# Training step of a parallel attention and SwiGLU block: copies joined, operand tiles kept in a ring, and a 64-row partial product issued beside the score pair

## The chip, the cores and the metric

The kernel runs on one core of a Trainium2 chip, in one launch. A NeuronCore has five engines with an instruction queue each: PE (matrix multiply), ACT (ScalarE), DVE (VectorE), POOL (GpSimd) and SP (which here only issues DMAs). Each engine works through its queue in order, and engines wait for each other by semaphores. The metric is device time in microseconds (us); lower is better. "Before" is the median of three runs.

## The reference

For x, dy of 2048 rows and 448 features (bfloat16), with 16 heads of 28 features and an FFN of 1792:

```
xn  = (x - mean) / sqrt(var + 1e-5)                # no gain, no bias
out = x + softmax(q k^T / sqrt(28)) v @ wo         # q, k, v = heads of xn @ wqkv
        + (silu(xn @ w_gate) * (xn @ w_up)) @ w_down
```

The outputs are `out` and the gradients of it, for the incoming `grad_out` (dy), with respect to x, wqkv, wo, w_gate, w_up and w_down.

## The kernel before

The 16 heads are 4 groups (`g`) of 4 heads; a head is padded from 28 to 32 rows, so a group fills 128 partitions. Rows of the sequence are 16 tiles (`t`) of 128. The 448 features are three chunks of 128 and one of 64 that is filled up with zeros; `xn_sp` and `dy_sp` hold rows with 512 columns, `xnT` and `dyT` the transposed chunks, and the weights `wq_sb`, `wgu`, `wdT` four chunks each with zeros in rows 64 to 127 of the last.

**Prologue.** x is loaded and normalised in four blocks (`ln_stats`, `ln_rows`), transposed on PE (`ln_columns`), and group 0 is projected (`proj_block`).

**Forward** (loop over `steps`: 4 groups, 4 query chunks `qc` of 512, 16 key tiles `kt`, so 256 steps). A step has two halves. In each, two score matmuls of 32 rows (L554) fill a two-bank PSUM tile and ACT takes its exp (L558). After the first half PE does the four PV matmuls of the step before last (`pv`, L536). Then `fill(pace)` issues other work from `queue` up to a budget, `pace = left / steps to go`: the FFN products (gate `a`, up `u`, and `dh` against dy; four 512-column matmuls each, L362), the weight gradients (`dW_items`, 16 matmuls of 448 columns each, L336), the projections of the next group (`proj_items`), and what follows from a finished query chunk (`o_items`). Each item is a list of (cost, function) pairs; `cur` is the one under way. The products and weight gradients share three PSUM buffers `f_ps`; DVE and ACT take the results out. Transposed copies are made by DMA; operands of the backward go to DRAM (`qT_d`, `spq_d` and so on), as do the FFN's hidden values and gradients (`hd_d`). After the last step the rest of the queue is issued and the forward's pools are closed.

**Backward** (loop over 512 `units` in 64 windows of 8; a unit is a pair of heads, a key chunk `kc` of 512 and a query tile). `load_pair` and `load_group` bring a pair's and a group's operands from DRAM, two buffers each (`qdp`, `spg`). Unit k: two score matmuls (L821, rows 0 to 63), two matmuls for d of the unit before (L834, rows 64 to 127), exp on ACT (L839), ds = d * E on DVE (L851), and four accumulating matmuls for the unit three back (`acc_mm`, L714). Six of eight ds tiles in a window are transposed by DMA, two (`TQ`) on PE into `aux` (L741): one at position 6 and one at position 0 of the next window. `tr_out` copies each out, the first half by ACT (L748), the second by DVE (L750). Each window also has one entry of `jobs` in positions 1 to 4, which needs the only `aux` buffer: a row tile of `out` (`y`, 21 matmuls), a row tile of the FFN's input gradient (`dx`, 14), a piece of the gradient of wqkv (`dwq`), or none. Position 5 has the dq matmuls (`dq_mm`).

**End.** The last group's `dwq`, then for each row tile 14 matmuls that sum the parts of the gradient of xn (`pab` and `dq_c`), and the LayerNorm's backward: `g_sb`, `junk`, `bb`, `cc` and `t2` on DVE, `t1` on ACT, `dx` on POOL, and the store.

All order is written out by hand (`manual_schedule`); the tile pools place the semaphores.

Of the kernel before, what the change touches and what calls it, by code (L numbers as in the profile page):

```python
# [37 lines left out]
def kernel(  # L38
# [53 lines left out]


    bst = ExitStack()
    bp = bst.enter_context(tc.tile_pool(name="bp", bufs=1))
    osp = bst.enter_context(tc.tile_pool(name="osp", bufs=2))
# [7 lines left out]
    qkp = bst.enter_context(tc.tile_pool(name="qkp", bufs=2))  # L104
    vp = bst.enter_context(tc.tile_pool(name="vp", bufs=1))
    stg = bst.enter_context(tc.tile_pool(name="stg", bufs=1))
    ep = bst.enter_context(tc.tile_pool(name="ep", bufs=7))
    op_ = bst.enter_context(tc.tile_pool(name="op_", bufs=1))
# [18 lines left out]
    for c, (d0, dn) in enumerate(DCH):  # L127
        act.dma_start(out=wst[:dn, c, :], in_=A_wqkv[d0:d0 + dn, :])
# [7 lines left out]
    dve.memset(xn_sp[:, :, D:], 0.0)  # L136
    dve.memset(wq_sb[64:, 3], 0.0)
# [4 lines left out]
    for w in wgu:  # L142
        pool.memset(w[64:, :, 3, :], 0.0)
    pool.memset(wd3[:, :, 64:], 0.0)
    pool.memset(dy_sp[:, :, D:], 0.0)
# [3 lines left out]
    for c, (d0, dn) in enumerate(DCH):  # L149
        pool.tensor_copy(  # L150
            out=wq_sb[:dn, c].rearrange("p t g (hh r) -> p t (g hh) r", r=HP)[:, :, :, :DH],
            in_=wst[:dn, c, :].rearrange("p (t h d) -> p t h d", t=3, h=H))

    def load_ffn_w(fc):
        w, fs = wgu[fc % 2], slice(fc * P, (fc + 1) * P)
        q = sp if fc < 2 else pool
        for i, src in enumerate((B_w_gate, B_w_up)):
            q.dma_start(out=w[:, i, 0:3, :], in_=src[0:384, fs].rearrange("(c p) f -> p c f", p=P))
            q.dma_start(out=w[:64, i, 3, :], in_=src[384:448, fs])
        sp.dma_start_transpose(out=wdT[fc % 2][:, 0:3, :], in_=B_w_down[fs, 0:384])  # L160
        sp.dma_start_transpose(out=wdT[fc % 2][:, 3:4, :], in_=wd3[:, fc, :])

    sp.dma_start(out=wd3[:, :, 0:64], in_=B_w_down[:, 384:448].rearrange("(fc p) d -> p fc d", p=P))
    load_ffn_w(0)
    for b in range(2):
        sp.dma_start(out=dy_sp[:, 8 * b:8 * b + 8, :D], in_=dy_d[:, 8 * b:8 * b + 8, :])
# [8 lines left out]

    def proj_unit(g, tq, sc, evac):

        key = (g, tq)
        if sc == 0:
            qk_tiles[key] = (vp if tq == 2 else qkp).tile([P, S], BF16, name=("qT", "kT", "vT")[tq])  # L180
        dst = qk_tiles[key]
        pp = ps_f.tile([P, 512], FP32, name="f_ps")

        def mm(c):
            pe.matmul(pp[:], lhsT=wq_sb[:, c, tq, g, :], rhs=xnT[:, 4 * sc:4 * sc + 4, c, :],
                      start=(c == 0), stop=(c == 3))
            if c < 3:
                return
            o = dst[:, sc * 512:(sc + 1) * 512]
            if tq == 0:  # L190
                if evac == "act":
                    act.copy(out=o, in_=pp[:])
                else:
                    dve.tensor_copy(out=o, in_=pp[:])
            elif evac == "act":
                act.activation(out=o, in_=pp[:], func=ACT.Identity, bias=r_ones[:, 0:1], scale=1.0)
            else:
                dve.tensor_scalar(out=o, in0=pp[:], scalar1=r_ones[:, 0:1], scalar2=None, op0=ALU.add)
        return mm
# [26 lines left out]
    def ln_rows(b):  # L226
        bs = slice(4 * b, 4 * b + 4)
        dve.reciprocal(out=rstd[:, bs], in_=rstd[:, bs])
        for t in range(4 * b, 4 * b + 4):
            dve.tensor_scalar(out=xn_sp[:, t, :D], in0=x_b[b][:, t % 4, :],  # L230
                              scalar1=mv[:, t, 0:1], scalar2=rstd[:, t:t + 1],
                              op0=ALU.subtract, op1=ALU.mult)

# [38 lines left out]
    spp = fst.enter_context(tc.tile_pool(name="spp", bufs=2))  # L272
    def weight_layout(c, i):
# [5 lines left out]
               else wq_sb[:dn, c].rearrange("p t g r -> p (t g r)"))  # L279
# [6 lines left out]
    cur = deque()  # L286
    left = [0.0]

    def fill(budget):

        while budget > 0.05:
            if not cur:
                if not queue:
                    return
                cur.extend(queue.popleft())
            cost, fn = cur.popleft()
# [3 lines left out]

    def push(jobs, front=False):
        left[0] += sum(c for job in jobs for c, _ in job)
# [5 lines left out]
    def proj_items(g):  # L308
        out = []
        for tq in range(3):  # L310
            for sc in range(4):
                box = {}

                def go(c, tq=tq, sc=sc, box=box):
                    if c == 0:
                        box["m"] = proj_unit(g, tq, sc, "dve")
                    box["m"](c)
                out.append([(MM, lambda c=c, go=go: go(c)) for c in range(4)])
# [36 lines left out]
    def ffn_items(fc, sc, extra):  # L355
# [3 lines left out]
        def mm(name, w, src, c):  # L359
            if c == 0:  # L360
                st[name] = ps_f.tile([P, 512], FP32, name="f_ps")
            pe.matmul(st[name][:], lhsT=w(c), rhs=src[:, tsl, c, :], start=(c == 0), stop=(c == 3))  # L362

        def a(c):
# [4 lines left out]
            mm("a", lambda c: wgu[fc % 2][:, 0, c, :], xnT, c)  # L369
# [12 lines left out]
        def u(c):  # L382
            mm("u", lambda c: wgu[fc % 2][:, 1, c, :], xnT, c)
# [7 lines left out]
        def dh(c):  # L391
            mm("dh", lambda c: wdT[fc % 2][:, c, :], dyT, c)
# [11 lines left out]
        def four(f):  # L404
            return [(MM, lambda c=c: f(c)) for c in range(4)]
        return [four(a), four(u)] + extra + [four(dh)]
# [3 lines left out]
    for fc in range(NFC):  # L410
        nxt = dW_items(fc)
        for sc in range(4):
            ffn_list += ffn_items(fc, sc, pend[sc - 1:sc] if sc else [])
# [4 lines left out]
        pend = nxt  # L418
    ffn_list += pend
# [25 lines left out]
    def o_items(g, qc, o_ps):  # L445
# [5 lines left out]
        if qc == 0:  # L451
            O_sp[g] = osp.tile([P, NT, P], BF16, name="O_sp")
# [68 lines left out]


# [19 lines left out]
    for i, (g, qc, kt) in enumerate(steps):  # L542
# [7 lines left out]
        for half in range(2):  # L550
            s_ps = ps_s.tile([P, 2, 512], FP32, name="s_ps")
            for j in range(2):
# [3 lines left out]
                          start=True, stop=True, tile_position=(r, 0))  # L556
            e = ep.tile([P, 2, 512], BF16, name="eT")
            act.activation(out=e[:], in_=s_ps[:], func=ACT.Exp, scale=SCALE)  # L558
            eTs[i].append(e)
            if half == 0 and i >= 2:  # L560
                pv(i - 2)
        pv_next[0] = max(0, i - 1)
# [17 lines left out]
    qdp = ast.enter_context(tc.tile_pool(name="qdp", bufs=2))  # L580
    spg = ast.enter_context(tc.tile_pool(name="spg", bufs=2))
# [11 lines left out]
    qd, spt, chunk, dsp, dqacc = {}, {}, {}, {}, {}  # L593

    def load_pair(pr, parts):

        g, r = pr // 2, 64 * (pr % 2)
        q = qdp.tile([P, S], BF16, name="QD")
        k = qdp.tile([P, S], BF16, name="KV")
        qd[pr] = (q, k)  # L600
        n = S // parts
        return [lambda i=i, dst=dst, r0=r0, src=src: sp.dma_start(
                    out=dst[r0:r0 + 64, i:i + n], in_=src[g, r:r + 64, i:i + n])
                for r0, srcs in ((0, (qT_d, kT_d)), (64, (dOT_d, vT_d)))
                for dst, src in zip((q, k), srcs) for i in range(0, S, n)]

    def load_group(g, parts):
        spt[g] = [spg.tile([P, NT, P], BF16, name=nm) for nm in ("Qsp", "Ksp", "dOsp")]
        n = NT // parts
        return [lambda i=i, t=t, src=src: sp.dma_start(  # L610
                    out=t[:, i:i + n, :].rearrange("p t c -> p (t c)"), in_=src[g, :, i * P:(i + n) * P])
                for t, src in zip(spt[g], (spq_d, spk_d, spo_d)) for i in range(0, NT, n)]


    jobs = [("y", t) for t in range(NT)] + [None, None] + [("dwq", 0, c) for c in range(4)]
# [19 lines left out]
    def dwq_mms(g, c, ps):  # L635
# [14 lines left out]
        for f in (kvm, qm):  # L650
            out += [lambda t=t, f=f: f(t) for t in range(NT)]
# [17 lines left out]
    def job_mms(i, ps):  # L669
        j = jobs[i]  # L670
        if j[0] == "dwq":
            return dwq_mms(j[1], j[2], ps)
# [71 lines left out]
    def tr_out(eng):  # L744

        ps, dst = st["tr"]
        if eng is act:
            act.copy(out=dst[:, 0], in_=ps[:, 0:4, :])  # L748
        else:
            dve.tensor_copy(out=dst[:, 1], in_=ps[:, 4:8, :])  # L750
# [43 lines left out]
    for f in load_pair(0, 1) + load_group(0, 1):  # L794
        f()
# [4 lines left out]
    for k in range(N + 2 * UW):  # L800
        W, pos = k // UW, k % UW
        if k < N:
# [3 lines left out]
            if k % 128 == 3 and pr + 2 < NPR:  # L806
                gload.extend(load_group(pr // 2 + 1, 2))
# [17 lines left out]
        if late_tr:  # L825
            pe_transpose(W - 1, TQ[1])
        if 1 <= k <= N:
# [4 lines left out]
            for j in range(2):  # L832
# [3 lines left out]
                          start=True, stop=True, tile_position=(r, 0))  # L836
        if k < N:
            E[k] = ework.tile([P, 2, 512], BF16, name="E")
            act.activation(out=E[k][:], in_=s_ps[:], func=ACT.Exp, scale=SCALE)  # L839
        if late_tr:  # L840
            tr_out(act)
            tr_out(dve)
# [33 lines left out]
        if pos == 6 and W < NW:  # L876
            pe_transpose(W, TQ[0])
            tr_out(act)
# [6 lines left out]
    with ExitStack() as fin:  # L885
# [4 lines left out]
        act.dma_start(out=dy_t[:], in_=dy_d)  # L890
        pab = [one.tile([P, NT, D], BF16, name=f"pab{i}") for i in range(2)]
        for i, src in enumerate((pA_d, pB_d)):
            for hf in range(2):
                sp.dma_start(out=pab[i][:, 8 * hf:8 * hf + 8, :], in_=src[:, 8 * hf:8 * hf + 8, :])  # L894
        dq_c = {}

        def load_c(ck):
            if ck < NT // 2:
                dq_c[ck] = ckf.tile([P, 3 * G, 2 * P], BF16, name="dq_c")
                sp.dma_start(out=dq_c[ck][:], in_=dqkv_d[ck])  # L900
        load_c(0)
        load_c(1)
        for c in range(4):
            ps = ps_sd.tile([P, 2, 512], FP32, name="sd")
            for f in dwq_mms(3, c, ps[:, 0, :]):
                f()
            dwq_out(3, c, ps[:, 0, :])
        wq = wtile["wq"]
        for t in range(NT):
# [7 lines left out]
            for n in range(3 * G):  # L917
                pe.matmul(g_ps, lhsT=cks[:, n, (t % 2) * P:(t % 2 + 1) * P], rhs=wq[:, n, :],  # L918
                          start=False, stop=(n == 3 * G - 1))
            g_sb = wk.tile([P, D], FP32, name="g_sb")  # L920
            s1 = wk.tile([P, 1], FP32, name="s1")
            dve.tensor_scalar(out=g_sb[:], in0=g_ps, scalar1=1.0, scalar2=None, op0=ALU.mult, op1=ALU.add,  # L922
                              accum_out=s1[:])
            junk = wk.tile([P, D], FP32, name="junk")
            s2 = wk.tile([P, 1], FP32, name="s2")
            dve.scalar_tensor_tensor(out=junk[:], in0=g_sb[:], scalar=1.0, in1=xn_sp[:, t, :D],  # L926
# [8 lines left out]
            act.activation(out=t1[:], in_=g_sb[:], func=ACT.Identity, scale=rstd[:, t:t + 1], bias=bb[:, 0:1])  # L935
# [37 lines left out]
```

## Time and profile before

| what | us |
|---|---|
| median of three runs | 1615.76 |
| lowest and highest run | 1614.84, 1618.48 |
| the profiled execution | 1618.11 |
| its span, first to last instruction | 1616.3 |

| engine | busy us | share of the span |
|---|---|---|
| PE | 1478.7 | 91% |
| DVE | 1121.4 | 69% |
| ACT | 1171.4 | 72% |
| POOL | 395.8 | 24% |

The first score matmul of the forward starts at 38.5 us of the span, its last matmul of any kind at about 688, the backward's first at 694.7, and the first matmul of the end's row tiles at 1551.5. In a line of the timeline the columns are the start, the time, the engine, the line of the kernel, the operation, the tile written and the tiles read, shapes, the number of merged instructions, and in brackets the idle time of the engine before it with what ended it. PE's durations overlap (a matmul is shown until its results are out), so for PE the distance of starts tells the time that it takes.

### The profile page before, as it was taken

The numbers are of one execution on the slowest core, as the hardware profiler recorded it, in microseconds if no ns is written. First come the engines' busy times: TensorE is split into PE (matmuls) and PEld (weight loads), VectorE is DVE, ScalarE is ACT, GpSimd is POOL, SyncE is SP. The second block draws the span as 40 slices with busy tenths as digits, with TensorE's granted clock in tenths as the row PEclk, the third lists the DMA queues.
The fourth block names the chain that finished last, engine by engine and source line by source line (L and its number), as shares of the span: only waits on it lengthen the run. The fifth ranks groups of instructions, "written<-read, shape, count | busy, mean of one in ns | idle before, by whom it ended". The sixth has DMA issues, their size and how long they took to land. (4 is left out here: it accounts for less than half of the span.)

```text
span 1616.3 us, 32124 instructions
## 1 busy us (share of the span) xinstructions
PE 1478.7 (91%) x12176; PEld 618.9 (38%) x12176; DVE 1121.4 (69%) x1526; ACT 1171.4 (72%) x1353; POOL 395.8 (24%) x662
## 2 busy tenths in 40 slices
PE   4999999999999999969999998999999899999784
PEld 2233333333333333323443344334345344544352
DVE  4664555566556666458877887888888788888645
ACT  4887888788788878547776777778777787777411
POOL 3322433243424463311010111101112011110132
PEclk9999999999999999989999999999999999999898
DMA  8965659766957796589999999999999999999962
GB/s 194 197 151 121 125 110 174 149 142 123 189 130 155 145 194 138 138 237 211 209 205 199 180 184 205 203 196 208 208 189 205 191 200 181 175 194 190 188 235 86
DMA packets 682283, 285.13 MB, mean 176 GB/s; under 512 B 637920, under 2 KB 651216, under 8 KB 682128
## 3 DMA queue, kind: packets, MB, share of 16 engines
q1 hardware_dynamic: 653472, 215.51, 71.8%
q0 software_dynamic: 25808, 64.30, 16.1%
q10 hardware_dynamic: 2848, 3.27, 0.7%
q8 instruction: 95, 1.56, 0.4%
q14 instruction: 60, 0.49, 0.1%
HBM read 67.34 MB, written 63.44 MB: 81 GB/s over the span
## 5 line engine op out<-in xcount | busy, mean ns | idle before, releaser
L851 DVE TENSOR_TENSOR ds<-sd,E 128x1024 bf16<-128x1024 f32 x512 | 608.0, 1217 | 84.4 <-PE sd L834 38.8
L839 ACT ACTIVATE E<-sd 128x1024 bf16<-128x1024 f32 x512 | 520.2, 1031 | 195.2 <-PE sd L834 104.6
L558 ACT ACTIVATE eT<-s_ps 128x1024 bf16<-128x1024 f32 x512 | 496.8, 1022 | 117.3 <-PE s_ps L554 115.9
L821 PE MATMUL sd<-KV,QD 32*128 32x512 bf16 x1024 | 203.3, 394 | 20.5 <-DVE ds L851 10.5
L834 PE MATMUL sd<-KV,QD 32*128 32x512 bf16 x1024 | 204.0, 391 | 9.7 <-DVE ds L851 5.4
L714 PE MATMUL acc<-ds,Qsp 128*32 128x512 bf16 x1024 | 205.5, 397 | 1.2 <-DVE ds L851 1.2
L714 PE MATMUL acc<-E,dOsp 128*32 128x512 bf16 x1024 | 205.2, 397 | 0.0
L554 PE MATMUL s_ps<-qT,kT 32*128 32x512 bf16 x1024 | 200.7, 389 | 2.2 <-ACT eT L558 2.1
L401 POOL DMA_DIRECT2D hd_d<-fT x168 | 126.9, 768 | 25.4 <-DVE fT L386 9.0
L362 PE MATMUL f_ps<-xnT,wgu 128*128 128x512 bf16 x448 | 120.2, 384 | 5.0 <-DVE w_sb L388 4.9
L684 PE MATMUL aux<-W,ck 128*128 128x448 bf16 x448 | 108.0, 358 | 6.5 <-DVE dsT L750 6.5
L729 POOL DMA_DIRECT2D dqkv_d<-dkv_o x64 | 39.3, 619 | 295.1 <-ACT dkv_o L720 293.3
L554 PEld LDWEIGHTS <-kT 32*128 32x128 bf16 x1024 | 48.2, 91 | 161.2 <-issue 160.1
L821 PEld LDWEIGHTS <-QD 32*128 32x128 bf16 x1024 | 50.0, 91 | 151.6 <-issue 143.8
L536 PE MATMUL o_ps<-eT,v_sp 128*32 128x512 bf16 x1024 | 103.5, 395 | 0.0
L336 PE MATMUL f_ps<-xn_sp,f_sp 128*128 128x448 bf16 x448 | 100.4, 355 | 0.0
L750 DVE COPY dsT<-aux 128x512 bf16<-128x512 bf16 x128 | 54.3, 424 | 62.6 <-ACT dsT L748 62.4
L714 PEld LDWEIGHTS <-dOsp 128*32 128x32 bf16 x1024 | 50.5, 94 | 121.6 <-issue 118.7
L741 PE MATMUL aux<-ident_bf,ds 128*128 128x128 bf16 x1024 | 80.3, 223 | 12.9 <-DVE dq_acc L778 4.8
L834 PEld LDWEIGHTS <-QD 32*128 32x128 bf16 x1024 | 68.8, 91 | 51.7 <-issue 32.9
L336 PEld LDWEIGHTS <-f_sp 128*128 128x128 bf16 x672 | 58.2, 98 | 70.7 <-issue 21.9
L748 ACT COPY dsT<-aux 128x512 bf16<-128x512 bf16 x128 | 76.2, 595 | 11.0 <-PE aux L741 9.0
(133 smaller groups left out, 1762.6 us busy)
## 6 DMA issues: line engine op xcount, KB each, us to landing
hd_d<-fT POOLq DMA_DIRECT2D x168, 128.0 KB, 4.3
ck<-hd_d SPq DMA_DIRECT2D x32, 448.0 KB, 4.3
ck<-hd_d SPq DMA_DIRECT2D x16, 576.0 KB, 4.7
dsT<-ds SPq DMA_TRANSPOSE x384, 4.1
dq_c<-dqkv_d SPq DMA_DIRECT2D x8, 768.0 KB, 4.7
dqkv_d<-dkv_o POOLq DMA_DIRECT2D x64, 64.0 KB, 3.7
W<-wT_d SPq DMA_DIRECT2D x14, 224.0 KB, 4.0
out_dram<-dw_o POOLq DMA_DIRECT2D x28, 96.0 KB, 4.0
```

The lines of the kernel that those rows point to most:

```text
L336: pe.matmul(acc[:, :D], lhsT=src[:, 12 * (t // 4) + 4 * wi + t % 4, :], rhs=rhs[:, t, :D], start=(t == 0), stop=(t == NT - 1))
L362: pe.matmul(st[name][:], lhsT=w(c), rhs=src[:, tsl, c, :], start=(c == 0), stop=(c == 3))
L401: pool.dma_start(out=hd_d[tsl, :, G + NFC * wi + fc, :].rearrange("k p s -> p k s"), in_=o[:, wi, :].rearrange("p (k s) -> p k s", k=4))
L536: pe.matmul(o_ps[HP * hh:HP * (hh + 1), :], lhsT=v[:, kt, HP * hh:HP * (hh + 1)], rhs=e[hh // 2][:, hh % 2, :], start=(kt == 0), stop=(kt ...
L554: pe.matmul(s_ps[:, j, :], lhsT=kT[r:r + HP, kt * P:(kt + 1) * P], rhs=qT[r:r + HP, qc * 512:(qc + 1) * 512], start=True, stop=True, tile_ ...
L558: act.activation(out=e[:], in_=s_ps[:], func=ACT.Exp, scale=SCALE)
L684: return [lambda n=n: pe.matmul(ps[:, :D], lhsT=t[:, n, :], rhs=w[:, n, :], start=(n == 0), stop=(n == NFC - 1)) for n in range(NFC)]
L714: pe.matmul(acc[r:r + HP, :], lhsT=src[:, qt, 64 * hp + HP * j:64 * hp + HP * j + HP], rhs=m[:, j, :], start=(qt == 0), stop=(qt == NT - 1 ...
L821: pe.matmul(s_ps[:, j, :], lhsT=q[HP * j:HP * j + HP, qt * P:(qt + 1) * P], rhs=kv[HP * j:HP * j + HP, kc * 512:(kc + 1) * 512], start=Tru ...
L834: pe.matmul(d_ps[:, j, :], lhsT=q[r:r + HP, qt * P:(qt + 1) * P], rhs=kv[r:r + HP, kc * 512:(kc + 1) * 512], start=True, stop=True, tile_p ...
L839: act.activation(out=E[k][:], in_=s_ps[:], func=ACT.Exp, scale=SCALE)
L851: dve.tensor_tensor(out=DS[k - 1][:], in0=d_ps[:], in1=E[k - 1][:], op=ALU.mult)
```

## The change

It has several parts.

- **Layout of the last 64 features.** In the weights they go to rows 64 to 127 of the fourth chunk, with zeros in rows 0 to 63. In `xn_sp` and `dy_sp` the last 64 features stand twice, in columns 384 to 447 and 448 to 511, by one DVE copy for each LN block and two POOL copies.
- **64-row start of a product.** A product takes the fourth chunk first. `fill` issues it as a full 128-row matmul, as before. `beside_scores`, called after the first score pair of each step, looks whether the next item is an FFN or projection product and, if none is begun yet, issues its first matmul with the 64 rows alone (tile position (64, 0)); `fill` takes the other three later.
- **dW of the last chunk.** In the last FFN chunk the pending weight gradients are placed one product later, and one goes to the end of the list.
- **Ring of operands.** The pools `qkp` and `vp` stay open through the backward; `load_pair` and `load_group` use the forward's tiles, and the first pair and group are loaded during the last head group. `jobs` starts with a window without a job.
- **Copies.** `tr_out` copies all eight blocks by one engine: DVE at position 6, ACT at position 0, where the transposes now come after d.
- **End.** `dwq` of group 3 does all dkv parts, then all dq parts; `pab` and `dy` are loaded by pieces with `dq_c`; `g_sb` is made by ACT, and `junk` and `t1` read PSUM.

```diff
-    qkp = bst.enter_context(tc.tile_pool(name="qkp", bufs=2))
-    vp = bst.enter_context(tc.tile_pool(name="vp", bufs=1))
+    qkp = ctx.enter_context(tc.tile_pool(name="qkp", bufs=2))
+    vp = ctx.enter_context(tc.tile_pool(name="vp", bufs=1))
...
-            q.dma_start(out=w[:64, i, 3, :], in_=src[384:448, fs])
+            q.dma_start(out=w[64:, i, 3, :], in_=src[384:448, fs])
...
-        sp.dma_start(out=dy_sp[:, 8 * b:8 * b + 8, :D], in_=dy_d[:, 8 * b:8 * b + 8, :])
+        ts = slice(8 * b, 8 * b + 8)
+        sp.dma_start(out=dy_sp[:, ts, :D], in_=dy_d[:, ts, :])
+        pool.tensor_copy(out=dy_sp[:, ts, D:], in_=dy_sp[:, ts, D - 64:D])
...
+    def feature_mm(ps, w, src, sc, c, beside):
+
+        if c == 0 and beside:
+            pe.matmul(ps[:], lhsT=w[64:, 3, :], rhs=src[64:, 4 * sc:4 * sc + 4, 3, :], start=True, stop=False,
+                      tile_position=(64, 0))
+        else:
+            pe.matmul(ps[:], lhsT=w[:, (c + 3) % 4, :], rhs=src[:, 4 * sc:4 * sc + 4, (c + 3) % 4, :],
+                      start=(c == 0), stop=(c == 3))
...
+        dve.tensor_copy(out=xn_sp[:, bs, D:], in_=xn_sp[:, bs, D - 64:D])
...
+    def wide(f):
+
+        return [(MM, lambda: f(0), lambda: f(0, True))] + [(MM, lambda c=c: f(c)) for c in range(1, 4)]
+
+    def beside_scores():
+
+        if begun or not queue or len(queue[0][0]) < 3:
+            return
+        begun.extend(queue.popleft())
+        cost, _, fn = begun.popleft()
+        fn()
+        left[0] -= cost
...
-            ffn_list += ffn_items(fc, sc, pend[sc - 1:sc] if sc else [])
+            k = sc - 1 if fc < NFC - 1 else sc - 2
+            ffn_list += ffn_items(fc, sc, pend[k:k + 1] if k >= 0 else [])
...
-        pend = nxt
-    ffn_list += pend
+        last, pend = pend[2:], nxt
+    ffn_list += last + pend
...
+            if half == 0:
+                beside_scores()
             e = ep.tile([P, 2, 512], BF16, name="eT")
             act.activation(out=e[:], in_=s_ps[:], func=ACT.Exp, scale=SCALE)
...
+        if g == G - 1 and qc == 2:
+            if kt == 0:
+                first = load_pair(0, 1) + load_group(0, 1, vp)
+            elif kt % 2 and first:
+                first.pop(0)()
...
-    jobs = [("y", t) for t in range(NT)] + [None, None] + [("dwq", 0, c) for c in range(4)]
+    jobs = [None] + [("y", t) for t in range(NT)] + [None] + [("dwq", 0, c) for c in range(4)]
...
-        if eng is act:
-            act.copy(out=dst[:, 0], in_=ps[:, 0:4, :])
-        else:
-            dve.tensor_copy(out=dst[:, 1], in_=ps[:, 4:8, :])
+        out, in_ = dst.rearrange("p j c q -> p (j c) q"), ps[:]
+        act.copy(out=out, in_=in_) if eng is act else dve.tensor_copy(out=out, in_=in_)
...
-        if late_tr:
-            pe_transpose(W - 1, TQ[1])
         if 1 <= k <= N:
...
                           start=True, stop=True, tile_position=(r, 0))
+        if late_tr:
+            pe_transpose(W - 1, TQ[1])
...
         if late_tr:
             tr_out(act)
-            tr_out(dve)
...
             pe_transpose(W, TQ[0])
-            tr_out(act)
             tr_out(dve)
...
+            if ck % 2 == 0:
+                ts = slice(2 * ck, 2 * ck + 4)
+                for i, src in enumerate((pA_d, pB_d)):
+                    sp.dma_start(out=pab[i][:, ts, :], in_=src[:, ts, :])
+                act.dma_start(out=dy_t[:, ts, :], in_=dy_d[:, ts, :])
...
+        for part in range(2):
+            for c, (ps, m) in enumerate(mms):
+                for f in m[part]:
+                    f()
+                if part == 1:
+                    dwq_out(3, c, ps)
...
-            dve.tensor_scalar(out=g_sb[:], in0=g_ps, scalar1=1.0, scalar2=None, op0=ALU.mult, op1=ALU.add,
-                              accum_out=s1[:])
+            act.activation(out=g_sb[:], in_=g_ps, func=ACT.Identity, accum_out=s1[:])
...
-            dve.scalar_tensor_tensor(out=junk[:], in0=g_sb[:], scalar=1.0, in1=xn_sp[:, t, :D],
+            dve.scalar_tensor_tensor(out=junk[:], in0=g_ps, scalar=1.0, in1=xn_sp[:, t, :D],
...
-            act.activation(out=t1[:], in_=g_sb[:], func=ACT.Identity, scale=rstd[:, t:t + 1], bias=bb[:, 0:1])
+            act.activation(out=t1[:], in_=g_ps, func=ACT.Identity, scale=rstd[:, t:t + 1], bias=bb[:, 0:1])
```

## The prediction

> **What bounds the kernel now.** The profiled execution took 1618.1 us: a span of 1616.3 and 1.8 around it. That is 2.3 above the median of the runs (1615.8); I work in the profile's time and put the difference on the median. The runs lie 3.6 apart (0.23%), so 0.2% is about what a measurement here can tell from no change.
>
> I first read the windows view (engine busy time by stretch), to see who is full in which stage.
>
> ```profile
> core 0: us, PE busy (x) PEld busy (x) DVE busy (x) ACT busy (x) POOL busy (x), PEclk, DMA share, GB/s
> 500.00:600.00 100.00, 96.74 (x614) 36.76 (x612) 61.87 (x108) 78.14 (x86) 44.12 (x64) 1.00 0.80 155
> 1400.00:1500.00 100.00, 97.65 (x951) 42.41 (x950) 88.55 (x91) 78.81 (x95) 12.97 (x26) 1.00 1.07 188
> 1552.00:1617.00 65.00, 42.24 (x221) 21.00 (x218) 38.90 (x112) 12.16 (x16) 18.23 (x23) 0.88 0.30 98
> ```
>
> The forward (41 to 688 us) is PE's: nothing else is near full. In the backward (695 to 1530) PE and DVE are both high, so the order within a window decides. At the end nobody is full: a chain of waits. Then the timeline of PE in the forward, one step and a product:
>
> ```profile
> 645.87 1.03 PE L362 MATMUL f_ps<-xnT,wgu 128*128 128x512 bf16 x4
> 646.83 0.39 PE L554 MATMUL s_ps<-qT,kT 32*128 32x512 bf16 x2
> ...
> 649.52 0.39 PE L554 MATMUL s_ps<-qT,kT 32*128 32x512 bf16 x2
> 649.84 0.40 PE L536 MATMUL o_ps<-eT,v_sp 128*32 128x512 bf16 x4
> 650.17 0.39 PE L554 MATMUL s_ps<-qT,kT 32*128 32x512 bf16 x2
> 650.49 1.88 PE L336 MATMUL f_ps<-xn_sp,f_sp 128*128 128x448 bf16 x9
> 652.30 0.39 PE L554 MATMUL s_ps<-qT,kT 32*128 32x512 bf16 x2
> ```
>
> Read the starts, not the durations. PE has no gap. A score pair stands 0.32, the four PV matmuls 0.33, the second pair 0.32. Nine 448-column fillers take 1.81, four of 512 columns 0.96. From starts inside such runs one 512-column matmul is 0.2135 and one of 448 columns 0.1875; what remains at each change from one tiling (32\*128, 128\*32, 128\*128) to another is 0.107. The same timeline in the backward and at the seam between the stages:
>
> ```profile
> 731.59 0.39 PE L821 MATMUL sd<-KV,QD 32*128 32x512 bf16 x2
> 731.60 0.39 PE L834 MATMUL sd<-KV,QD 32*128 32x512 bf16 x2
> 731.92 1.12 PE L678 MATMUL aux<-W,ck 128*128 128x448 bf16 x5
> ```
>
> ```profile
> 670.76 0.74 PE L336 MATMUL f_ps<-dy_sp,f_sp 128*128 128x448 bf16 x3 [2.61 <-DMA f_sp<-fT]
> ...
> 684.78 3.19 PE L425 MATMUL f_ps<-dy_sp,O_sp 128*128 128x448 bf16 x16
> 694.66 1.04 PE L821 MATMUL sd<-KV,QD 32*128 32x512 bf16 x4 [6.69 <-DMA KV<-kT_d]
> 696.88 0.61 PE L834 MATMUL sd<-KV,QD 32*128 32x512 bf16 x2 [1.18 <-DMA KV<-vT_d]
> 702.44 1.67 PE L678 MATMUL aux<-wo_pad,ck 128*128 128x448 bf16 x4 [4.95 <-DMA ck<-hd_d]
> ```
>
> Four 32-row matmuls in four row groups take 0.32, as two do. At the seam PE waits for loads three times. Last, the waits in 740 to 1500 us, and DVE at the end:
>
> ```profile
> DVE dsT L750 <- ACT dsT L748: 58.5, 118, 1.0
> ```
>
> ```profile
> 1560.65 1.02 DVE L926 SCALAR_TENSOR_TENSOR junk<-g_sb,xn_sp 128x448 f32<-128x448 f32 x1
> ...
> 1562.58 0.68 DVE L937 SCALAR_TENSOR_TENSOR t<-xn_sp,cc,t 128x448 f32<-128x448 bf16 x1 [0.71 <-ACT t L935]
> 1563.18 0.62 DVE L922 TENSOR_SCALAR_CACHE_REDUCE g_sb<-sd 128x448 f32<-128x448 f32 x1
> ```
>
> **The change part by part.**
>
> **1. The 64-row part beside the scores.** Stepping through the code's queue (costs and paces as written, 256 steps, one chance each, only when a product stands next) gives 128 of the 204 FFN and later projection products begun beside a pair: 27 gate, 29 up, 50 dh, 22 projection. The others pay four full matmuls as now. No row shows a 64-row matmul beside 32-row ones. Lower end: it rides along free, as L834 does beside L821 (other row groups, other banks), and 128 x 0.2135 = 27.3 us of filler leave PE. Upper end: 64 rows are another tiling, PE closes the pair first, and each such product costs 0.2135 + 0.107 beside the pair in place of 0.2135: 128 x 0.107 = +13.7. The first gate matmul of a chunk also issues the next chunk's weight loads (four on POOL, two transposes on SP), at most a step earlier than now, with a chunk of some 45 us to land: nothing. I take the lower end: L821 and L834 are the nearest rows in what matters, disjoint rows of the array. A tenth goes to ACT: two exps start 0.91 apart, so a step needs 1.83 plus tanh there, and steps 16 to 32 already last only 2.15 (starts of the exps). **-24.6.**
>
> The Trainium skill (TensorEngine Tiling (Array Packing), Key Properties) says that a change of tiling mode, not just of tile, drains the array, and lists 64-row and 32-row tilings as different modes. The 0.107 at each change agrees with it; whether it holds between disjoint row groups, no run here shows.
>
> **2. dW of the last FFN chunk** now has one older dW item ahead of it: 16 matmuls, 3.0 us plus the scores between them, longer than the 2.61 wait for f_sp. **-2.6.**
>
> **3. The seam.** Pair 0 and group 0 are loaded in the last head group, seven loads of 0.5 us on SP's queue, one every second step, into buffers whose readers ended a group earlier; behind them stand only forward transposes with that slack. The first window has no job, so nothing waits for ck. First exp: 0.4 after PE's last forward matmul (688.0) in place of 695.4: -7.0. First window: 19.0 now (695.4 to 714.4, the starts of every eighth exp); by the same starts the three windows without a job last 12.9 to 13.5: -6.1. The jobless window is taken from the two after the y rows: 13.5 becomes 12.6, -1.0. Bounds -8 (the ds ring filling while transposes wait) to -17. **-14.1.**
>
> **4. Copies of transposed ds.** Now each half waits in turn: ACT 0.60, then DVE 0.42. After, DVE alone copies at position 6, ACT alone at position 0, and there d goes ahead of the transposes. ACT's 1024 columns cost 1.03 (E's row has that size), DVE's about 0.7 (0.42 plus 512 columns' share). The loop that sets a dx window (12.02) runs from the job's first matmul (1412.11): PE 8.49 to the last unit's scores (1420.60), ACT's copy and two exps, a copy by ACT and one by DVE, next job 1424.13. After: PE 8.35 (the 0.28 wait for a ds at position 2 halves); exp of the last unit +0.4, since ACT copies nothing there; next exp +0.91; full copy +0.91, 1.03 long; +0.05 to PE: 11.7 to 11.8. So -0.2 per dx, dwq and jobless window, 47 of them; in y windows (12.57) PE's 21 matmuls lead, and d waiting for its exp takes back what is won: 0. DVE's 58.5 us of waits mostly turn into waits for PE. Bounds: -25 (half of them return) to +6 (d's wait counts in each window). **-9.4.**
>
> **5. The end.** dwq of group 3 now runs all dkv parts before the dq parts, filling the 5 us in which PE waited for dq_sp: it ends near 1543 in place of 1549.3. dq_c comes behind 0.9 MB of pab, not 3.7: the wait to 1551.46 (16.7 us after issue) goes: -8.4. In the loop g_sb moves from DVE to ACT; DVE's round falls from 3.30 to 2.53 (1560.65 to 1563.18, still with its 0.71 for ACT) and PE's 14 matmuls (2.65) lead: 0.63 x 15 = -9.5. Loads of pab and dq_c stand behind the out writes on SP's queue, which wait for dx; by that they have some 6.6 us to land 2.2 MB, at two of the eight chunks: +2. ACT issues dy in four pieces of 0.4 each between its copies, in time that it has idle. Bounds -8 to -18. **-15.9.**
>
> **6. Prologue.** Each LN block gets a DVE copy ahead of its last transposes, about 0.8 on the first block, later ones behind projections. The wo_pad loads on POOL's queue now stand behind a copy that waits for dy (about 24 us instead of 12.7); their user starts at 47.5. **+0.8** (0 to 2).
>
> Sum: -24.6 - 2.6 - 14.1 - 9.4 - 15.9 + 0.8 = -65.8, so 1550.0.
>
> **Rivals.** *The tilings don't run together*: part 1 is +13.7, the rest stays: -27.5, 1588.3. For it: every change of tiling in the trace costs 0.107. Against: all those changes reuse the rows just in use. *Slower*: the early start claims one of three f_ps buffers a product sooner, and PE stands in front of PV and the second pair until DVE has evacuated. The three such waits in 60 to 660 us (f_ps L362 for w_sb) are 1.6 on average. From 43 of the 128 on, this eats all gains; if all 56 gate and up starts wait, +90: 1640. Against: DVE is 62% busy and mostly a dW of 16 matmuls stands between. *Window order*: d, held for its exp at position 0, now has the transposes, the acc matmuls and through them ACT's copy and the job behind it. If that costs 0.5 in all 63 windows on top of the first rival, -27.5 + 31.5 = +4: 1620; it decides from 0.49 a window on.
>
> **How the numbers follow.** Chances: forecast 0.56 (own range 1534 to 1566), tilings apart 0.34 (1572 to 1604), buffers 0.07, window order 0.03. The range 1536 to 1596 takes in both large cases less their outer tails and leaves out the slower two. Faster 0.90, same 0.02, slower 0.08.
>
> **What would show it.** Right: a score pair, a 64x512 matmul and PV start within 0.33 of each other; forward end near 661 us; first backward exp 0.4 later; 11.8 in dx windows; final rounds of 2.65. Wrong: PV 0.64 after the pair; waits of f_ps for DVE; first exps waiting for a DMA; PE waiting for pab at the end.

## The result, and the profile after

The kernel after takes 1596.7 us (median of 4 runs, 1592.3 to 1599.3) beside 1617.1 for the kernel before on the same chip (4 runs, 1614.8 to 1622.8): a ratio of 0.987, 95% interval 0.983 to 0.990. It is faster by 1.3%, about 20 us in place of the 66 forecast, and the median lies 0.7 above the upper end of the range. The profiled execution took 1592.3, a span of 1590.6. Its stages, by the starts of the exps and of PE's matmuls, against the span of before (us):

| stage | before | after | change | forecast |
|---|---|---|---|---|
| to the first forward exp | 40.6 | 42.0 | +1.4 | +0.8 |
| forward, to PE's last dW matmul | 647.4 | 657.6 | **+10.2** | **-27.2** |
| seam, to the start of backward window 1 | 26.4 | 11.9 | -14.5 | -13.1 |
| windows 1 to 62 | 792.6 | 789.6 | -3.0 | -10.4 |
| window 63 and dwq of group 3, to the first dq_c matmul | 44.4 | 35.1 | -9.3 | -8.4 |
| last loop, to the end | 64.9 | 54.3 | -10.6 | -7.5 |
| sum | | | -25.8 | -65.8 |

Most of the miss is one stage, the forward, which became longer; some 7 of it lie in the windows of the backward.

The windows view of the kernel after, in stretches like those shown of before (the last stage now begins some 16 us earlier):

```profile
core 0: us, PE busy (x) PEld busy (x) DVE busy (x) ACT busy (x) POOL busy (x), PEclk, DMA share, GB/s
500.00:600.00 100.00, 97.12 (x599) 35.42 (x598) 58.54 (x99) 80.84 (x88) 40.98 (x60) 1.00 0.70 138
1400.00:1500.00 100.00, 96.53 (x946) 41.34 (x944) 89.10 (x85) 81.84 (x89) 14.38 (x29) 1.00 1.08 194
1540.00:1591.00 51.00, 38.95 (x204) 19.50 (x201) 27.67 (x80) 20.55 (x46) 19.43 (x27) 0.92 0.50 170
```

PE is as full in the forward as before (97.1 and 96.7 of 100), so it still sets the stage; that the stage is longer says that PE's work has not become less. The timeline of PE in the forward of the kernel after, one start of a product beside a score pair (start, us, line, tile, tiling):

```profile
608.49 0.39 PE L600 MATMUL s_ps<-qT,kT 32*128 32x512 bf16 x2
608.81 0.39 PE L178 MATMUL f_ps<-dyT,wdT 64*128 64x512 bf16 x1
609.12 0.40 PE L582 MATMUL o_ps<-eT,v_sp 128*32 128x512 bf16 x4
609.46 0.39 PE L600 MATMUL s_ps<-qT,kT 32*128 32x512 bf16 x2
609.78 1.50 PE L359 MATMUL f_ps<-dy_sp,f_sp 128*128 128x448 bf16 x7
```

Read the starts. The pair stands 0.32, the 64-row matmul 0.31, PV follows at 609.12: 0.63 after the pair. Had the 64-row matmul run together with the pair, PV would have started at 608.81. The trace holds 128 such matmuls, as the stepping through the queue had given; for the 108 of them that stand at full clock with no wait before them, the median from the pair to the next matmul is 0.64.

The seam and the last loop in the timelines of the kernel after, first PE, then DVE in three consecutive rounds:

```profile
696.41 3.19 PE L447 MATMUL f_ps<-dy_sp,O_sp 128*128 128x448 bf16 x16
700.32 0.39 PE L850 MATMUL sd<-kT,qT 32*128 32x512 bf16 x2 [0.71 <-DVE dwd_sb L463]
...
1552.17 2.43 PE L954 MATMUL sd<-W,dq_c 128*128 128x448 bf16 x12
1554.44 0.54 PE L952 MATMUL sd<-pab,ident_bf 128*128 128x448 bf16 x2
1554.82 2.43 PE L954 MATMUL sd<-W,dq_c 128*128 128x448 bf16 x12
```

```profile
1549.67 0.69 DVE L972 SCALAR_TENSOR_TENSOR t<-xn_sp,cc,t 128x448 f32<-128x448 bf16 x1 [0.85 <-ACT t L970]
...
1552.41 0.69 DVE L972 SCALAR_TENSOR_TENSOR t<-xn_sp,cc,t 128x448 f32<-128x448 bf16 x1 [0.85 <-ACT t L970]
...
1555.14 0.69 DVE L972 SCALAR_TENSOR_TENSOR t<-xn_sp,cc,t 128x448 f32<-128x448 bf16 x1 [0.85 <-ACT t L970]
```

The first backward scores no longer wait for a load (6.69 before, 0.71 now, for DVE). In the last loop PE's round is 2.65, as forecast, but DVE's is 2.73, with 0.85 of waiting for ACT in it. Last, the waits of 740 to 1480 us, before and after (total, times, longest):

```profile
DVE ds L851 <- DMA dsT<-ds: 28.7, 26, 3.3
```

```profile
DVE ds L879 <- DMA dsT<-ds: 56.3, 43, 3.3
DVE ds L879 <- PE sd L861: 45.2, 99, 5.0
```

DVE's wait for ACT's half of the copy is gone, as meant. In its place DVE waits twice as long as before for the transfers that transpose ds (a ds buffer is free when its transfer has landed), and longer for PE (18.5 before). How the two share it differs between executions: the kernel without the start beside the scores, below, has the same backward and windows of the same length, with 35.4 for the transfers and 54.7 for PE.

### The profile page after: what moved, and what is told of

The parts are those of the page before. It is cut to its first block, busy times and chain, and to the rows that moved or that the text cites. A ratio compares the mean times of both kernels' runs of the same rounds, so it can differ in the third digit from the quotient of the medians.

```text
span 1590.6 us, 31990 instructions
## 1 busy us (share of the span) xinstructions
PE 1456.6 (92%) x12176; PEld 604.8 (38%) x12176; DVE 1102.5 (69%) x1433; ACT 1194.0 (75%) x1321; POOL 395.4 (25%) x663
## 4 chain that ended last, share of the span: by engine, by line
PE 61%; DMA 14%; DVE 9%; ACT 9%; issue 4%; POOL 1%; SPq 1%; DVEq 0%; POOLq 0%; ACTq 0%
DMA dsT<-ds 10%; PE s_ps L600 8%; PE f_ps L181 8%; PE f_ps L359 8%; PE sd L850 5%; ACT E L868 5%; PE aux L717 4%; PE o_ps L582 4%; DVE ds L879 4%; PE acc L747 4%; PE aux L774 3%; PE aux L794 3%; ACT dsT L781 3%; PE sd L861 2%; PE aux L711 2%
## 5 line engine op out<-in xcount | busy, mean ns | idle before, releaser
L879 DVE TENSOR_TENSOR ds<-sd,E 128x1024 bf16<-128x1024 f32 x512 | 610.9, 1220 | 135.3 <-DMA dsT<-ds 58.2
L606 ACT ACTIVATE eT<-s_ps 128x1024 bf16<-128x1024 f32 x512 | 503.6, 1023 | 119.3 <-PE s_ps L600 118.3
L861 PE MATMUL sd<-kT,qT 32*128 32x512 bf16 x1024 | 202.2, 388 | 23.1 <-ACT E L868 22.4
L850 PE MATMUL sd<-kT,qT 32*128 32x512 bf16 x1024 | 201.3, 390 | 23.4 <-DVE ds L879 21.0
L747 PE MATMUL acc<-ds,v_sp 128*32 128x512 bf16 x1024 | 204.5, 394 | 0.7 <-DVE ds L879 0.7
L747 PE MATMUL acc<-E,O_sp 128*32 128x512 bf16 x1024 | 204.3, 394 | 0.2 <-ACT dkv_o L753 0.2
L181 PE MATMUL f_ps<-xnT,wgu 128*128 128x512 bf16 x392 | 106.6, 385 | 4.3 <-DVE w_sb L411 4.3
L850 PEld LDWEIGHTS <-qT 32*128 32x128 bf16 x1024 | 51.0, 91 | 152.0 <-issue 143.6
L747 PEld LDWEIGHTS <-O_sp 128*32 128x32 bf16 x1024 | 50.3, 93 | 112.6 <-issue 103.0
L774 PE MATMUL aux<-ident_bf,ds 128*128 128x128 bf16 x1024 | 79.9, 221 | 11.7 <-DVE dq_acc L806 7.5
L861 PEld LDWEIGHTS <-qT 32*128 32x128 bf16 x1024 | 65.5, 91 | 61.3 <-issue 57.0
L369 DVE CAST dwT<-f_ps 128x448 bf16<-128x448 f32 x28 | 17.5, 625 | 96.1 <-PE f_ps L359 96.1
L794 PE MATMUL aux<-dsT,vT 128*32 128x512 bf16 x1024 | 75.7, 393 | 5.0 <-DMA dsT<-ds 3.6
```

The lines of the kernel that those rows point to most:

```text
L181: pe.matmul(ps[:], lhsT=w[:, (c + 3) % 4, :], rhs=src[:, 4 * sc:4 * sc + 4, (c + 3) % 4, :], start=(c == 0), stop=(c == 3))
L747: pe.matmul(acc[r:r + HP, :], lhsT=src[:, qt, 64 * hp + HP * j:64 * hp + HP * j + HP], rhs=m[:, j, :], start=(qt == 0), stop=(qt == NT - 1 ...
L774: pe.transpose(ps[:, i, :], ds[:, i // 4, (i % 4) * P:(i % 4 + 1) * P], ident_bf[:])
L850: pe.matmul(s_ps[:, j, :], lhsT=q[HP * j:HP * j + HP, qt * P:(qt + 1) * P], rhs=kv[HP * j:HP * j + HP, kc * 512:(kc + 1) * 512], start=Tru ...
L861: pe.matmul(d_ps[:, j, :], lhsT=q[r:r + HP, qt * P:(qt + 1) * P], rhs=kv[r:r + HP, kc * 512:(kc + 1) * 512], start=True, stop=True, tile_p ...
L879: dve.tensor_tensor(out=DS[k - 1][:], in0=d_ps[:], in1=E[k - 1][:], op=ALU.mult)
```

## The experiments

Eight kernels, in two groups that each ran beside the kernel before on one chip; before took 1618.2 and 1615.1 there. The kernel after is in neither group, so between it and the others the ratios compare better than the medians. "Forward" is the second stage of the table above. The granted clock is the share of PE's full speed that the trace shows; 0.50 and 1.00 are its only values here. "At full clock" takes half of each stretch at 0.50 away, so it is an estimate of what the same work takes without such stretches. W are backward windows by the starts of every eighth exp. Stages are those of one profiled execution.

| kernel | median us | ratio to before, 95% | forward | at full clock | seam | W1-5 | W51-62 | last loop |
|---|---|---|---|---|---|---|---|---|
| before | 1617.1 | | 647.4 | 635.4 | 26.4 | 65.6 | 145.5 | 64.9 |
| after | 1596.7 | 0.987 (0.983-0.990) | 657.6 | 652.5 | 11.9 | 71.9 | 143.4 | 54.3 |
| before, 64-row start alone | 1622.9 | 1.003 (0.999-1.006) | 659.1 | 652.3 | 26.4 | 65.3 | 145.5 | 62.7 |
| after, no start beside scores | 1591.8 | 0.984 (0.979-0.988) | 651.7 | 634.7 | 11.7 | 71.0 | 143.3 | 60.7 |
| after, 32-row start | 1579.8 | 0.977 (0.972-0.982) | 643.8 | 623.3 | 11.9 | 71.1 | 143.3 | 55.0 |
| after, copies as before | 1605.2 | 0.991 (0.987-0.994) | 661.0 | 652.5 | 12.0 | 71.7 | 145.5 | 56.9 |
| after, transposes first | 1598.5 | 0.988 (0.982-0.995) | 657.8 | 651.0 | 11.7 | 73.3 | 140.7 | 58.2 |
| after, no start, transposes first | 1591.8 | 0.984 (0.979-0.990) | 655.9 | 635.4 | 11.7 | 72.4 | 140.7 | 57.9 |
| after, seam undone | 1598.9 | 0.989 (0.984-0.994) | 661.9 | 651.7 | 20.9 | 65.3 | 143.3 | 57.8 |
| after, g_sb on DVE | 1599.2 | 0.990 (0.983-0.996) | 659.9 | 651.3 | 11.9 | 75.0 | 143.3 | 62.9 |

**Part 1 taken out of the kernel after.**

```diff
-            if half == 0:
-                beside_scores()
```

> The changed kernel without the call after the first score pair: no product is begun beside a pair, all 204 take four 128-row matmuls from the queue; everything else of the change stays. Theory 1 (the 64-row and the 32-row tilings do not run together, so a start beside the pair costs 0.31 to 0.32 us of PE in place of 0.2135): 128 starts x 0.1 = 13 us back, and of the 10 us of waits for f_ps behind DVE some 5 more; the forward ends at 681 to 687 us of the span in place of 699.6, the whole is 1573 to 1582 where the changed kernel's profiled run had 1592. Theory 2 (the starts are free and the forward became longer by waits of the single f_ps ring and of ACT): the forward is set by its waits, so it stays within 5 us of 699.6. Theory 3 (the starts do save PE time, something else of the change made the forward longer): it gets longer by up to 27 us.

Measured: forward end at 694.1, not 681 to 687, and 1591.8 for the run, not 1573 to 1582. The direction is that of the theory that the tilings don't run together; the size is masked by the clock. At full clock the forward is 17.8 shorter than after's (634.7 and 652.5), but this kernel has 34 us of the forward at half clock, after 10. The windows view of the forward, after first, then this kernel, shows it as a mean clock of 0.99 and 0.97:

```profile
42.00:699.60 657.60, 631.56 (x3911) 228.60 (x3911) 375.50 (x649) 530.97 (x569) 247.44 (x360) 0.99 0.74 151
```

```profile
42.30:694.10 651.80, 628.46 (x3911) 232.88 (x3911) 374.89 (x649) 522.16 (x569) 247.18 (x360) 0.97 0.75 152
```

Where the slow stretches stand can be read in the trace: all but the first, at the stage's start, lie beside a gap of PE of 1.8 to 3.9 us. Without the early start PE comes to the transposes of o_raw sooner and stands; the longest of its waits in 60 to 660 us, in the waits view of this kernel:

```profile
PE f_ps L479 <- DVE o_raw L470: 18.6, 10, 3.9
```

With the start this wait is 1.0 in all. So some of what PE saves is lost in that wait and in slower matmuls behind it. For the whole run the gain is not shown: the two ratios, 0.984 and 0.987, have overlapping intervals.

**The start with 32 rows in place of 64.** It leaves out half of the last 64 features in the 128 products begun early; the tiling is now that of the scores.

```diff
-            pe.matmul(ps[:], lhsT=w[64:, 3, :], rhs=src[64:, 4 * sc:4 * sc + 4, 3, :], start=True, stop=False,
+            pe.matmul(ps[:], lhsT=w[64:96, 3, :], rhs=src[64:96, 4 * sc:4 * sc + 4, 3, :], start=True, stop=False,
```

> The changed kernel, with one edit: the matmul beside the first pair takes 32 rows (64 to 95) in place of 64, so it has the same tiling as the scores. Those 128 products leave out half of the last 64 features; instructions, order and queue are the same. Theory 1 (a change of tiling drains PE, equal tilings in other rows run together): first pair, 32-row matmul and PV start within 0.32 to 0.34 us in place of 0.63, 128 x 0.31 = 40 us of PE time less, less what ACT (1.83 us of exps in a step) and waits for f_ps take back: forward end at 662 to 675 in place of 699.6, whole 1555 to 1568. Rival (PE takes no third matmul beside a pair, whatever its tile): PV still starts 0.63 after the pair, whole 1590 to 1596.

The timeline of PE of this kernel, one step:

```profile
599.95 0.39 PE L600 MATMUL s_ps<-qT,kT 32*128 32x512 bf16 x2
599.96 0.38 PE L178 MATMUL f_ps<-xnT,wgu 32*128 32x512 bf16 x1
600.27 0.40 PE L582 MATMUL o_ps<-eT,v_sp 128*32 128x512 bf16 x4
600.60 0.39 PE L600 MATMUL s_ps<-qT,kT 32*128 32x512 bf16 x2
```

The start lies 0.01 behind the pair and PV begins 0.32 after the pair: it costs PE nothing. Nothing but the number of rows, and with it the tiling, differs from the kernel after, so that decides, not the place, the bank or the order. The forward at full clock is 12.1 shorter than before's and 29.2 shorter than after's, of the 40 that the sum gave. It ends at 686.0, later than the 662 to 675 expected (and the run takes 1579.8, not 1555 to 1568), for two reasons that the trace shows: 41 us of it at half clock, and more waiting for f_ps, in the waits view of this kernel above all

```profile
PE f_ps L178 <- DVE w_sb L411: 14.8, 8, 4.6
```

All waits of PE for f_ps and o_ps in the forward are 29.6 here, 24.5 after and 20.5 before; so 5 of the missing 11 are such waits, and the rest was not traced. The prediction's rival of the three f_ps buffers is thus real, but worth 4 to 9 us and not 90.

**Part 1 alone on the kernel before**, with its layouts; every other part is left as before.

```diff
...
+            if half == 0:
+                beside_scores()
```

> The kernel before with part 1 alone: the 64-row start beside the score pair, with the layouts it needs; the seam, the copies, dW's order and the end stay as before. Theory 1 (the 64-row tiling does not run together with the 32-row one and costs one more change of tiling): 128 x 0.107 = +13.7 at full clock, and some waits for f_ps; forward from first exp to end 654 to 664 in place of 647, the run 1622 to 1636. Rival (the start itself is worth what it saves, and another part of the joined change lengthens the forward): forward at or below 647, the run 1590 to 1617.

Measured: 1622.9, ratio 1.003 (0.999 to 1.006), forward 659.1, inside the first theory's 654 to 664. At full clock it is 652.3, as in the five other kernels of the study that begin products with 64 rows (651.0 to 652.5); the three that don't have 634.7 to 635.4. So the start with 64 rows costs the forward +17: 128 x 0.107 = 13.7 for the change of tiling, and 4.3 of additional waits for f_ps and o_ps (24.8 and 20.5) come close to it. The clock gives some of it back: 13.7 us at half clock in place of 23.9, where PE's wait of f_ps for o_raw has fallen from 12.2 to 1.8. So the stage grows by 11.7 and the whole run by about a quarter of a per cent, at the edge of what can be measured.

**Copies of transposed ds split again** (each half by its own engine, transposes ahead of d), the rest as after.

```diff
-        act.copy(out=out, in_=in_) if eng is act else dve.tensor_copy(out=out, in_=in_)
+        if eng is act:
+            act.copy(out=dst[:, 0], in_=ps[:, 0:4, :])
+        else:
+            dve.tensor_copy(out=dst[:, 1], in_=ps[:, 4:8, :])
...
         late_tr = pos == 0 and 1 <= W <= NW
+        if late_tr:
+            pe_transpose(W - 1, TQ[1])
...
         if late_tr:
             tr_out(act)
+            tr_out(dve)
...
+            tr_out(act)
             tr_out(dve)
```

> The changed kernel with both copies split again between ACT and DVE, and the transposes ahead of d, as before the change. If the prediction's part 4 is right in size: quiet dx windows 12.0 and 12.23 again in place of 11.78 and 12.05, whole +9 us. Rival (faster windows only wait more for the DMA transposes of ds, 56 us of DVE waits now against 29 before): DVE waits for them 25 to 35 us and the whole is within 4 us.

Measured: the undisturbed dx windows go from 11.78 and 12.05 (they alternate) back to 12.00 and 12.23, windows 51 to 62 from 143.4 to 145.5, and windows 1 to 62 together from 789.6 to 796.4. Part 4 is worth 6.7 in the windows of the profiled executions, beside the 9.4 of the forecast. The medians differ by 8.5, but they come from different groups, and the two ratios (0.991 and 0.987) have overlapping intervals: the gain is shown for the windows, not for the whole run.

**Only the transposes back ahead of d**, once in the kernel after and once in the kernel without the start.

```diff
+        if late_tr:
+            pe_transpose(W - 1, TQ[1])
         if 1 <= k <= N:
...
-        if late_tr:
-            pe_transpose(W - 1, TQ[1])
```

> The changed kernel with the late transposes at position 0 again ahead of d, the copies by one engine kept. If the loop through PE, two exps and ACT's copy sets a window, as the prediction worked it: d's wait for its exp is filled by the transposes, -0.2 us in the quiet dx windows (11.78 and 12.05 become 11.55 and 11.8) and about as much in y windows, -10 to -13 us in all. Rival (the DMA transposes of ds set the pace, DVE waits for them 56 us): quiet windows get shorter, the disturbed ones longer, within 4 us in all.

> The kernel after without the start beside the scores, and with the transposes of ds ahead of d at position 0. Theory A (undisturbed windows add up): 0.2 less in each of 47 windows than without the start alone, 1580 to 1585. Theory B (windows in which loads and transposes meet, and stretches at half clock, take it back): undisturbed dx windows 11.56 and 11.83 as in the run with the transposes first, the excess of the others 8 to 12 larger, the run 1588 to 1596.

Measured: undisturbed dx windows of 11.56 and 11.83, another 0.22 less, in both kernels; windows 51 to 62 take 140.7. So the mechanism of the rival on the window order is real (d, held for its exp, holds the transposes), at 0.22 a window and not 0.5. Yet the runs are no faster: 1598.5 beside 1596.7, and 1591.8 without the start, the same as with d first; there windows 1 to 62 together take 789.5 for 788.6. Windows 1 to 5 are 1.4 longer in both, and the stretches at half clock within windows 1 to 62, at half of their length, come to 24 and 19 us in place of 11 and 14. That is theory B of the second run; why shorter windows bring more half clock than they save was not settled.

**The seam undone**: the loads of the first pair and group go out at the start of the backward, as before; the job order stays as after.

```diff
-        if g == G - 1 and qc == 2:
-            if kt == 0:
-                first = load_pair(0, 1) + load_group(0, 1, vp)
-            elif kt % 2 and first:
-                first.pop(0)()
...
+    for f in load_pair(0, 1) + load_group(0, 1, vp):
+        f()
     job_load(0)
```

> The kernel after, with the loads of the first pair and group issued at the start of the backward again. Theory: the first backward exp comes 6 to 8 later, the first window is some 4 to 6 longer than 10.7 because its operands land one after the other: forward end to second window 22 to 25 in place of 11.9, the run 1603 to 1612. Rival (what the seam gains is lost again in the windows behind it, where PE and DVE then wait for transposes on SP's queue): the windows after the first become shorter by as much, the run 1592 to 1600.

PE's timeline at the seam of this kernel shows the wait that the early loads remove:

```profile
710.81 1.04 PE L847 MATMUL sd<-kT,qT 32*128 32x512 bf16 x4 [7.27 <-DMA kT<-kT_d]
713.19 0.61 PE L858 MATMUL sd<-kT,qT 32*128 32x512 bf16 x2 [1.35 <-DMA kT<-vT_d]
```

The seam is 9.0 longer (20.9 and 11.9, where 22 to 25 were expected), but the run only 2.2 (1598.9), and the two ratios overlap. The waits of DVE in windows 1 to 5, the kernel after first, then this one:

```profile
DVE ds L879 <- DMA dsT<-ds: 13.1, 9, 2.6
```

```profile
DVE ds L876 <- DMA dsT<-ds: 4.0, 2, 2.7
```

In the same windows of before it is 0.7. Windows 1 to 5 take 65.3 to 65.6 in the three kernels that load at the seam, and 71.0 to 75.0 in all seven that load early. The rival holds: 6.6 of the 9.0 that the seam gains are lost in the next five windows, and DVE waits there for transfers. That the transfers are the limit is likely, not shown. All three kernels move 211 to 214 GB/s in windows 1 to 5, but after moves 15.2 MB there, before 13.9 and this kernel 14.0; at that rate 1.2 MB more are an estimated 5.5 us. The busy share of the 16 DMA engines tells less: it is 0.9 or more in nearly all of 740 to 1480, before and after, undisturbed windows included. The clock has a part as well: after has 11.5 us of windows 1 to 5 at half clock and this kernel 4.8, so by half of these stretches about half of the 6.6 us is slower matmuls.

**g_sb on DVE again**, in 32 bits, in the last loop; `junk` and `t1` read it again in place of PSUM.

```diff
-            act.activation(out=g_sb[:], in_=g_ps, func=ACT.Identity, accum_out=s1[:])
+            dve.tensor_scalar(out=g_sb[:], in0=g_ps, scalar1=1.0, scalar2=None, op0=ALU.mult, op1=ALU.add,
+                              accum_out=s1[:])
...
-            dve.scalar_tensor_tensor(out=junk[:], in0=g_ps, scalar=1.0, in1=xn_sp[:, t, :D],
+            dve.scalar_tensor_tensor(out=junk[:], in0=g_sb[:], scalar=1.0, in1=xn_sp[:, t, :D],
...
```

> The kernel after, with g_sb written by DVE in 32 bits again in the last loop. Theory (DVE's round of three operations sets the loop): 0.63 more in each of some 15 rounds, first to last 62 to 65 in place of 54.3, the run 1601 to 1608. Rival (the loop waits for pab and dq_c by the queue, whoever writes g_sb): 54 to 57, the run 1594 to 1600.

DVE in its last loop:

```profile
1582.46 0.62 DVE L958 TENSOR_SCALAR_CACHE_REDUCE g_sb<-sd 128x448 f32<-128x448 f32 x1
1583.12 1.02 DVE L962 SCALAR_TENSOR_TENSOR junk<-g_sb,xn_sp 128x448 f32<-128x448 f32 x1
1585.78 0.62 DVE L958 TENSOR_SCALAR_CACHE_REDUCE g_sb<-sd 128x448 f32<-128x448 f32 x1
```

DVE's rounds without a wait for PE are 3.31 to 3.32 (1582.46 to 1585.78 is one) against 2.73, and the loop takes 62.9 against 54.3. So DVE's round sets the loop when it carries g_sb: 0.58 in each of 15 rounds is 8.7. The rounds show this, not the length of the loop. In the seven kernels with g_sb on ACT the loop takes 54.3 to 60.7, much of the difference being one round of 4.0 to 8.0 in the middle, in which DVE stands behind PE's wait for operands, and after's is the shortest. The median, 1599.2, is below the expected 1601 to 1608, and its four runs spread over 20 us (1590.2 to 1610.3, the profiled one being the longest): the gain is shown for the rounds, not for the whole run.

## Why the prediction was wrong, point by point

**Part 1: the step that failed.** The sum took the lower end, free as L834 beside L821, with "disjoint rows of the array" as what matters. What matters is the tiling. Two 32-row matmuls in disjoint rows run together; a 64-row and a 32-row one in disjoint rows don't, and each start pays 0.2135 + 0.107 (0.31 to 0.32 by the starts). That is the upper end, +13.7, and the first rival, given 0.34. The prediction had noted that every change of tiling in the trace costs 0.107 and set that aside because those changes reuse rows just in use; the 0.107 was the better row. The rule of the Trainium skill (TensorEngine Tiling (Array Packing), Key Properties) that a change of mode, not just of tile, drains the array would have given the right sign: the traces after and with 32 rows agree with it, at 0.63 and 0.32 from the pair to PV. At full clock the part cost +17 in place of -24.6.

**With that rival the sum was near, in part by luck.** It gave 1588.3 for the median, which is 1590.6 in the profile's time; the profiled execution took 1592.3, the median 1596.7. But the forward's +10.2, beside the rival's +11.1, is +17 at full clock less what the clock gave back (10.2 us at half clock in place of 23.9). And of the 7.4 that windows 1 to 62 fell short, 5.4 came back at the seam and the end, where the loop of this execution is the shortest of seven.

**Part 2: right in the wait, nothing in the sum.** The 2.61 wait for f_sp is gone. But the forward at full clock is only 0.7 and 0.0 shorter than before's in the two kernels that have this part and not the start, and 652.5 with both parts beside 652.3 with the start alone. In the last 54 us of the first kernel without the start PE waits 4.7 for o_raw, where before waited 0.8.

**Part 3: right in its stage, not in the whole.** -14.5 from the forward's end to window 1, -13.1 forecast. Its two terms are off by more, in opposite directions: the first exp came 1.3 after PE's last forward matmul, not 0.4 (-6.1 for -7.0), and the first window took 10.7, not 12.9 (-8.4 for -6.1). Then windows 1 to 5 took 6.3 more. The sum asked who waits at the seam, not what is late next. The bounds of -8 to -17 looked at the seam alone. The swap of the jobless window is mixed: it takes 10.8 in place of 13.5, but dwq's first job then reaches dq_sp too soon. Windows 17 and 18 together went from 25.8 to 28.2; PE's timeline after shows why:

```profile
948.63 0.96 PE L680 MATMUL aux<-dq_sp,xn_sp 128*128 128x64 bf16 x15 [4.00 <-DMA dq_sp<-dq_o]
```

**Part 4: right in the undisturbed windows.** Forecast 11.7 to 11.8 for a dx window (12.02 before); measured 11.78 and 12.05 for 12.00 and 12.23, and 12.48 and 12.54 for 12.57 and 12.60 in y windows, which had been put at 0. Splitting the copies again cost 6.7. All windows together gave only -3.0 of the -10.4, although they hold less half clock than before's (21.7 us in place of 37.5): windows 1 to 5 took 6.3 back, and the rest was not traced. DVE's waits of 56.6 for ACT did not mostly become waits for PE: in these executions 26.7 did, and 27.6 went to the transfers of ds.

**Part 5: right, the size of the loop in part by luck.** The dwq step -9.3 for -8.4; the loop -10.6 for -7.5, with rounds of 2.73, set by DVE and ACT, where 2.65 by PE were forecast. With loops of 55.0 to 60.7 the six other kernels with this end have -4 to -10. **Part 6:** +1.4 for +0.8.

## What to carry to other kernels

Here a small matmul rode along with another in the same tiling; in another tiling it cost its own time and one more change, although its rows were free. So look for a split that has the partner's shape, or leave it out. Two 32-row matmuls, in rows 64 to 95 and 96 to 127, would have that shape and leave nothing out, like the four in four row groups that the prediction shows for the backward; they were not run. Where a stall at the head of a stage is removed, look at the next windows: here 9 us of waiting at the seam came back as 6.6 us of longer windows, in which DVE waits for transfers. The kernel after without the start beside the scores is, with either order of the transposes, the fastest that leaves nothing out (1591.8, ratio 0.984), but its interval overlaps with that of the kernel after. At full clock its forward is 17.8 us shorter; in time it is 5.9.

## What the runs showed of the hardware that was not expected

- A 64x512 matmul in rows 64 to 127 waits for a 32-row pair in rows 0 to 63: 0.32 + 0.31 by the starts. A 32x512 one in rows 64 to 95 starts 0.01 after the pair, and PV 0.32 after it.
- Gaps of PE can cost more than their length. Between 60 and 690 us of five kernels looked at for this (before, after, after without the start, with the 32-row start, and before with the start alone), each stretch at a granted clock of 0.50 in the forward lay within 2 us of a PE gap of 1.2 to 4.6 us and lasted 3.4, 6.8 or 10.2 us; the score pairs then stand 0.53 instead of 0.32. By half of their length the forward lost an estimated 5 to 10 us in this way in the kernels with the 64-row start, 12 to 21 in the others. In the forwards of all ten kernels, from 60 us on, all 40 such stretches lie within 2 us of a gap; of the 77 gaps of 1.0 us and more 40 have one, all 13 above 2.7 us, none below 1.2, and some between. So it is a link, and no threshold was measured. The Trainium skill (TensorE: Matmul & The Clock Gate, Part 1) puts the half rate behind an idle window of about 3.4 us: the lengths agree with that as a unit, but shorter gaps were followed by it here.
